# Tile 0's keys from x by columns, centred by the mean's row, with 1/std applied behind the products

## The chip, the cores and the metric

The kernel runs on one core of one Trainium2 chip. The metric is the time of one launch on the device in microseconds (us), as the median of several runs. The engines of the core are TensorE (PE in the profile; PEld is its weight load), VectorE (DVE), ScalarE (ACT), GpSimd (POOL) and SyncE (SP), whose queue issues the DMAs of this kernel's early part. All times below that are not medians are on the clock of one profiled execution, counted from its first instruction.

## The reference, cut to what matters

The kernel computes x + A(layernorm(x)) + B(layernorm(x)) for 2048 tokens of width 512, where A is a linear attention block and B a mixture of experts with two experts of eight for each token. Only the keys and the gate's logits of A and B are touched here:

```python
def _layernorm(x, axis=-1, eps=1e-5):
    m = jnp.mean(x, axis=axis, keepdims=True)
    v = jnp.var(x, axis=axis, keepdims=True)
    return (x - m) / jnp.sqrt(v + eps)
...
xn = _layernorm(x, axis=-1)
...
phi = lambda t: jnp.where(t > 0, t + 1, jnp.exp(t)) + 1e-6
pq, pk = phi(q), phi(k)                       # k = xn @ wqkv[:, 512:1024]
kv = jnp.einsum("bhsd,bhse->bhde", pk, v)
z = jnp.einsum("bhsd->bhd", pk)
...
logits = xf @ w_gate                          # xf = xn
```

Since (x - m) / std times a weight is ((x - m) times the weight) / std for each token, the division by std may stand behind the product.

## The kernel before

The 2048 tokens are 16 tiles of 128 (`t` = 0 to 15). The first stage runs over the tiles on all engines at once. For a tile, DVE takes mean and variance (`ln_stat`: `bn_stats` into `bs`, then `bn_aggr` into `mv`); POOL adds epsilon and raises to the power -1/2 (`ln_pow`) and refines that to 1/std with the bias -mean/std (`ln_fin_g`: six small operations on `sm`, ending in `rs` and `nb`); ACT writes the normalized tokens `xn` (`ln_out`); PE transposes them to columns (`transp_pe`, tile `xtp`), and ACT and DVE split the columns into a rounded high part and a low rest (`transp_split`, tile `xnT`: `split_hi` on ACT, line 150, `split_lo` on DVE, line 153). PE then takes keys and logits from them in 24 products, three for each quarter of the width and each half of the weights (`k_proj`), the features `pk` of the keys are formed, split in two (`pkhl`, beside `xnhl` for the tokens), and PE adds their outer product to four accumulators (`g_acc`, `gacc`, 12 products of 512 columns).

Tiles 4 to 15 already go another way: their columns come ready from a transposed copy of x in memory (`xcols`, tile `xraw`), PE turns the means into a row (`means_pe`, tile `mrow`), DVE subtracts that row (`centre`), and ACT multiplies the products by `rs` as it forms the features. `TS` = 4 is the first such tile; for the tiles below it the constants `rneg`, `std` and `estd` are set by memsets (lines 270 to 272), and `scales` works them out for the others.

Tile 0 is the head of the kernel and is written out by hand (lines 780 to 820). Until its columns are there PE runs small products on ones (`keep_warm`, line 231). Its statistics, `va` and 1/std come on DVE (`ln_stat(0)`, `ln_pow` line 301, `ln_fin(0)`), DVE makes its `xn` in two halves (line 336), PE transposes these (`first_pe`), ACT and DVE split them (`first_hi`, `first_lo`; the latter reads PSUM). The weights of the keys come in four quarters (`wkst`, four DMAs on SP behind those of x tiles 0 and 1) and are split as they land (`wk_hi` on ACT, `wk_lo` on DVE, both reading SBUF). The products for tile 0 are issued in an order written out in `k_part` ((quarter, pass) pairs; pass 0 is high by high, 1 takes the low weights, 2 the low columns): `k1` for the first half of the key columns, `k2` for the second half and the gate. `transp_pe(1)` and `transp_split(1)` are issued within `k2`, `transp_pe(2)` within `g_acc(0)` behind its first four products.

The order on each engine is the order of the calls: the schedule is manual, and an engine does not pass an instruction that waits. So on DVE the statistics of tile 2 (`ln_stat(2)`) stand between the low parts of the third and fourth weight quarter, and on POOL the operations of `ln_pow` and `ln_fin_g` for tiles 1, 2, 3 follow one another. SP's queue is in order too: the writes of `xn` to `xn_d` (line 338) stand in it as issued, and the loads of x tiles 4 and 5 behind those of tiles 0 and 1.

## Time and profile before

| | us |
|---|---|
| median of 3 runs | 824.85 (824.60 to 825.12) |
| the profiled execution, as timed | 825.74 |
| its span, first to last instruction | 824.0 |
| PE busy in the span | 816.3 (99%) |
| DVE, ACT, POOL busy | 679.1, 554.0, 265.3 |

How to read the profile: a row of a timeline gives the start and the duration of one instruction or of several merged ones (x4: four), its engine, line, operation, the tile it writes and those it reads, and in brackets how long its engine sat idle before it and what released it. Successive instructions of one engine can overlap by about 0.1 us, since the next one starts before the last has drained. A line such as 153 belongs to a helper, so the tiles tell which use it is. Ends of matmuls are modelled.

### The profile page before, as it was taken

What the parts mean: (1) busy time and instruction counts of PE and PEld (TensorE: products, weight loads), DVE (VectorE), ACT (ScalarE), POOL (GpSimd) and SP (SyncE); (2) the same over time, 40 slices, a digit from 0 to 9 for tenths busy, and PEclk for the clock granted to TensorE, in tenths of its full rate; (3) what the DMA queues carried; (4) which work ended last, traced back from release to release, by engine and by line L of the source; (5) the groups of instructions that cost most, each with busy time, mean ns of one, the idle gap of its engine ahead of it and who ended that gap; (6) DMA issues with size and microseconds to landing.
All of it is one profiled execution on the core that took longest, in us unless ns stands there. A gap on an engine that the chain in (4) does not pass through costs nothing. (4 is left out here: it accounts for less than half of the span.)

```text
span 824.0 us, 15861 instructions
## 1 busy us (share of the span) xinstructions
PE 816.3 (99%) x5359; PEld 744.6 (90%) x5359; DVE 679.1 (82%) x1415; ACT 554.0 (67%) x1167; POOL 265.3 (32%) x380
## 2 busy tenths in 40 slices
PE   8999999999999999999999999999999999999997
PEld 8899888888999999999999999999999998888886
DVE  7898889989989777877887888788888888987851
ACT  5687574458777566667776777677767777776750
POOL 5675243465310600042505340451217023411011
PEclk9999999999999999999999999999999999999999
DMA  4861044465855843474648455745656464549507
GB/s 168 282 228 67 30 163 170 128 202 184 260 178 147 209 137 103 144 196 126 144 133 235 116 126 159 207 110 151 167 172 153 146 170 113 121 131 235 134 4 176
DMA packets 105498, 128.22 MB, mean 156 GB/s; under 512 B 14590, under 2 KB 68606, under 8 KB 105382
## 3 DMA queue, kind: packets, MB, share of 16 engines
q1 hardware_dynamic: 91526, 106.95, 42.7%
q0 software_dynamic: 12880, 18.66, 12.0%
q10 hardware_dynamic: 1008, 1.57, 0.6%
q8 instruction: 43, 0.70, 0.4%
q14 instruction: 41, 0.34, 0.1%
HBM read 97.23 MB, written 31.22 MB: 156 GB/s over the span
## 5 line engine op out<-in xcount | busy, mean ns | idle before, releaser
L1261 POOL DMA_INDIRECT out_dram<-yo,sidx x22 | 35.2, 1601 | 276.8 <-DVE yo L1256 272.5
L1261 POOL DMA_INDIRECT out_dram<-yu,L x47 | 77.9, 1657 | 92.4 <-ACT yu L1354 60.8
L153 DVE TENSOR_TENSOR h<-hs,h 128x512 fp32r<-128x512 f32 (+7 forms) x112 | 78.5, 701 | 5.5 <-ACT h L150 5.1
L150 ACT ACTIVATE h<-hs 128x512 fp32r<-128x512 f32 (+7 forms) x112 | 72.3, 646 | 3.2
L1412 ACT ACTIVATE hs<-px 128x288 f32<-128x288 f32 (+7 forms) x54 | 21.1, 390 | 55.1 <-PE px L1404 53.3
L1427 ACT ACTIVATE hs<-hs 128x288 f32<-128x288 f32 (+7 forms) x54 | 23.0, 427 | 45.9 <-DVE hs L1426 44.1
L1431 DVE TENSOR_TENSOR hs<-px,hs 128x288 f32<-128x288 f32 (+7 forms) x54 | 23.4, 434 | 34.0 <-PE px L1404 33.0
L1426 DVE TENSOR_TENSOR hs<-pz,hs 128x288 f32<-128x288 f32 (+7 forms) x54 | 23.3, 431 | 32.7 <-PE pz L1404 30.4
L500 PE MATMUL gacc<-pkhl,xnhl 128*128 128x512 f32 x192 | 48.0, 396 | 0.1
L1128 POOL DMA_INDIRECT xg<-xn_d,gidx x37 | 41.7, 1126 | 19.8 <-issue 7.6
L500 PEld LDWEIGHTS gacc<-pkhl,xnhl 128*128 128x128 f32 x192 | 34.8, 188 | 7.6 <-DVE pkhl L480 0.9
L1260 POOL MEMSET spacer<- 1x1 f32 x69 | 37.9, 550 | 7.3 <-issue 7.3
L1432 ACT ACTIVATE hs<-hs 128x288 f32<-128x288 f32 (+7 forms) x54 | 22.8, 422 | 18.0 <-DVE hs L1431 16.2
L1504 POOL TENSOR_TENSOR pz<-pq,den 128x512 f32<-128x512 f32 x16 | 17.3, 1084 | 53.5 <-DVE den L1503 52.3
L1437 DVE TENSOR_TENSOR hs<-py,hs 128x288 f32<-128x288 f32 (+7 forms) x54 | 23.0, 425 | 13.5 <-PE py L1404 12.7
L1473 ACT ACTIVATE e_q<-qp,rneg 128x512 f32<-128x512 f32 x16 | 11.0, 688 | 32.6 <-PE qp L1464 29.1
L1422 ACT ACTIVATE hs<-px 128x288 f32<-128x288 f32 (+7 forms) x54 | 21.2, 392 | 16.4 <-PE px L1404 13.8
L1285 PE MATMUL y<-w_5h,h 128*128 128x512 f32 (+2 forms) x88 | 32.0, 394 | 0.0
L1285 PE MATMUL y<-w_1h,h 128*128 128x512 f32 (+2 forms) x88 | 32.0, 393 | 0.0
L1285 PE MATMUL y<-w_2h,h 128*128 128x512 f32 (+2 forms) x88 | 32.0, 393 | 0.0
L1285 PE MATMUL y<-w_3h,h 128*128 128x512 f32 (+2 forms) x88 | 32.0, 393 | 0.0
L1285 PE MATMUL y<-w_4h,h 128*128 128x512 f32 (+2 forms) x88 | 31.7, 393 | 0.0
(699 smaller groups left out, 3177.5 us busy)
## 6 DMA issues: line engine op xcount, KB each, us to landing
wst<-in_B_w_dram SPq DMA_DIRECT2D x196, 128.0 KB
wst<-in_B_w_dram SPq DMA_DIRECT2D x36, 512.0 KB
zz<-in_B_w_dram SPq DMA_DIRECT2D x27, 512.0 KB
xs_d<-xg SPq DMA_DIRECT2D x119, 64.0 KB
xq<-xs_d SPq DMA_DIRECT2D x28, 256.0 KB
x<-in_A_x_dram SPq DMA_DIRECT2D x21, 256.0 KB
xn_d<-xn SPq DMA_DIRECT2D x16, 256.0 KB
xraw<-in_xcols_dram SPq DMA_DIRECT2D x6, 512.0 KB
```

Source lines behind the costliest of these rows:

```text
L150: A.activation(hi, src, AF.Copy)
L153: V.tensor_tensor(lo, src, raw(hi), op=ALU.subtract)
L500: T.matmul(gacc[d], xnhl[:, a, d * P:(d + 1) * P], pkhl[:, b, :], start=(t == 0 and i == 0), stop=(t == NT - 1 and i == 2))
L1128: G.indirect_dma_start(out=raw(t), out_offset=None, in_=xn_d, in_offset=IOA(ap=gidx[:, b:b + 1], axis=0))
L1260: G.memset(spacer, 0.0)
L1261: st = G.indirect_dma_start(out=rows, out_offset=IOA(ap=idx, axis=0), in_=src, in_offset=None, compute_op=ALU.add).ins
L1285: T.matmul(ya[r, d][:m], h[a][:, d * P:d * P + m], w[b][:, n % 2, :], start=(first and i == 0), stop=(last and i == 2))
L1426: V.tensor_tensor(c12, pz_, c12, op=ALU.add)
L1427: A.activation(c12, c12, AF.Silu)
L1431: V.tensor_tensor(c22, px, c22, op=ALU.add)
L1432: A.activation(c22, c22, AF.Silu)
L1437: V.tensor_tensor(c11, pz_, c11, op=ALU.add)
```

## The change

The load of tile 0's columns (`xraw0`, half of the first entry of `xcols`) is put behind that of x tile 0, and the load of x tile 1 behind the first weight quarter. In the head, PE turns the mean of tile 0 into a row and DVE subtracts it from `xraw0` in place; `cols_hi(0)` and `cols_lo(0)` split the result. DVE's `va` and `ln_fin` for tile 0 go to POOL (`ln_fin_g(0, 1)`, between the statistics of tile 1 and the POOL work of tile 1). `xn` of tile 0 is made by ACT (`ln_out(0, 0, 0, A)`), behind the split of tile 1's columns, and with it the statistics and POOL work of tile 2 move behind that split. Keys and logits of tile 0 are multiplied by `rs` as ACT reads them (`k_act0`, `k_feat0`: Exp, Relu and Identity with a scale, in place of two Exp and a chain on DVE). The fourth weight quarter is split ahead of `ln_out(1)`, `transp_pe(1)` moves back by four products, the first run of small products is shortened from 136 to 112 and the second changed from 3 of 128 columns to 31 of 40. `rneg`, `std`, `estd` of tile 0 are worked out like those of the tiles from 4 on.

```diff
--- before.py
+++ after.py
@@ -174,13 +174,16 @@
     wk2 = [um(f"wk2_{i}")[:, :KC * 264].rearrange("p (k f) -> p k f", k=KC) for i in range(2)]
     wk_st = []
     load_x(0)
-    load_x(1)
+    xraw0 = wp.tile([P, SW], F32, tag="s", name="xraw0", bufs=18)
+    Q.dma_start(xraw0[:, :D], xcols[0, :, :D])
     for c in range(2):
         w = (512, 528)[c]
         for i in range(2):
             st = raw(um(f"wkst{c}{i}"))[:, :w]
             Q.dma_start(st, wkg[:, 1024 * c + w * i:1024 * c + w * i + w])
             wk_st.append(((wk1_v, wk2)[c], i, st.rearrange("p (k f) -> p k f", k=2)))
+            if c == i == 0:
+                load_x(1)
     load_x(2)
     load_x(3)
 
@@ -237,7 +240,7 @@
         idt = raw(um("idt"))[:, :P]
         make_identity(nc, idt)
         V.tensor_copy(ident_r, idt)
-        keep_warm("warm", 136, 40)
+        keep_warm("warm", 112, 40)
 
     def constants_b():
         def iota(t, pattern, base=0, cm=0):
@@ -267,9 +270,9 @@
         for r in range(E):
             G.memset(i_cap[:, RANKS[r]:RANKS[r] + 1], float(CAP[r]))
         G.memset(gate, 0.0)
-        G.memset(rneg[:, :TS], -1.0)
-        G.memset(std[:, :TS], 1.0)
-        G.memset(estd[:, :TS], 1e-6)
+        G.memset(rneg[:, 1:TS], -1.0)
+        G.memset(std[:, 1:TS], 1.0)
+        G.memset(estd[:, 1:TS], 1e-6)
         for a in range(4):
             G.memset(part[a * BLK:(a + 1) * BLK], float(a))
         G.affine_select(out=lower, in_=ones[:, :E * E].rearrange("p (a b) -> p a b", a=E),
@@ -298,7 +301,7 @@
         sm = wp.tile([P, 4, 2], F32, tag="sm", name=f"sm{g}", bufs=4)
         va, r0, t0, nb = (sm[:, j, :n] for j in range(4))
         rf = rs[:, g:g + n]
-        (V if g == 0 else G).tensor_scalar(va, mv[:, :n, 1], EPS, None, op0=ALU.add)
+        G.tensor_scalar(va, mv[:, :n, 1], EPS, None, op0=ALU.add)
         G.tensor_tensor(r0, va, eps_t[:, :n], op=ALU.pow)
         lnst[g] = (mv, va, r0, t0, nb, rf)
 
@@ -320,9 +323,10 @@
         G.tensor_tensor(nb, nb, rf, op=ALU.mult)
 
     def scales():
-        V.reciprocal(std[:, TS:], rs[:, TS:])
-        G.tensor_scalar(rneg[:, TS:], rs[:, TS:], -1.0, None, op0=ALU.mult)
-        G.tensor_scalar(estd[:, TS:], std[:, TS:], 1e-6, None, op0=ALU.mult)
+        for c in (slice(0, 1), slice(TS, NT)):
+            V.reciprocal(std[:, c], rs[:, c])
+            G.tensor_scalar(rneg[:, c], rs[:, c], -1.0, None, op0=ALU.mult)
+            G.tensor_scalar(estd[:, c], std[:, c], 1e-6, None, op0=ALU.mult)
 
     def ln_out(g, i, t, eng):
         mv, va, r0, t0, nb, rf = lnst[g]
@@ -436,14 +440,19 @@
 
     pks = {}
 
-    def k_feat0(k1, k2):
-        pk, e = ta("pk0"), ta("e_k0")
-        for o, src in ((0, k1), (256, k2[:, :256])):
-            A.activation(e[:, o:o + 256], src, AF.Exp)
-        V.tensor_scalar(e, e, 1.0, 1e-6, op0=ALU.min, op1=ALU.add)
-        for o, src in ((0, k1), (256, k2[:, :256])):
-            V.scalar_tensor_tensor(pk[:, o:o + 256], src, 0.0, e[:, o:o + 256], op0=ALU.max, op1=ALU.add)
-        V.tensor_copy(L[:, 0, :], k2[:, 256:264])
+    first = []
+
+    def k_act0(i, k):
+        if i == 0:
+            first.extend((ta("pk0"), ta("r0")))
+        for dst, fn in zip(first, (AF.Exp, AF.Relu)):
+            A.activation(dst[:, 256 * i:256 * i + 256], k[:, :256], fn, scale=rs[:, 0:1])
+
+    def k_feat0(k2):
+        pk, r = first
+        k_act0(1, k2)
+        A.activation(L[:, 0, :], k2[:, 256:264], AF.Identity, scale=rs[:, 0:1])
+        V.scalar_tensor_tensor(pk, r, 1.0, pk, op0=ALU.add, op1=ALU.min)
         pks[0] = pk
         return pk
 
@@ -465,7 +474,7 @@
     def z_add(t):
         G.tensor_tensor(zacc, zacc if t > 1 else pks.pop(0), pks.pop(t), op=ALU.add)
         if t == 6:
-            G.tensor_scalar(zacc, zacc, (NT - 1) * 1e-6, None, op0=ALU.add)
+            G.tensor_scalar(zacc, zacc, NT * 1e-6, None, op0=ALU.add)
 
     def two_hi(name, src, eps=False):
         hl = tb(name).rearrange("p (h c) -> p h c", h=2)
@@ -779,44 +788,50 @@
 
     constants_a()
     ln_stat(0, 0, 0)
+    m0 = psk("mrow0")[:, 0, :P]
+    T.transpose(m0, lnst_mv[0][:, 0, 0:1].broadcast_to([P, P]), ident)
+    keep_warm("warm_b", 31, 40)
+    xc[0] = xraw0[:, :D]
+    x3 = xc[0].rearrange("p (k c) -> p k c", k=KC)
+    V.tensor_tensor(x3, x3, m0.unsqueeze(1).broadcast_to([P, KC, P]), op=ALU.subtract)
     ln_pow(0, 1)
-    wk_hi(0)
     ln_stat(1, 0, 1)
+    ln_fin_g(0, 1)
     ln_pow(1, 1)
     ln_fin_g(1, 1)
-    ln_fin(0, 1)
-    ln_out(0, 0, 0, V)
-    first_pe()
-    keep_warm("warm_b", 3)
-    first_hi()
+    cols_hi(0)
+    wk_hi(0)
+    cols_lo(0)
     wk_lo(0)
-    first_lo()
     wk_hi(1)
     wk_lo(1)
     wk_hi(2)
     wk_lo(2)
     k1 = psm("acc", "k1_0", 256)
-    k_part(k1, wk1_v, (0, 0), (1, 0), (0, 1), (1, 1), (0, 2), (1, 2),
+    k_part(k1, wk1_v, (0, 0), (1, 0), (0, 2), (1, 2), (0, 1), (1, 1),
            (2, 0), (3, 0), (2, 2), (3, 2), (2, 1), (3, 1))
+    wk_hi(3)
+    wk_lo(3)
     ln_out(1, 0, 1, A)
+    k_act0(0, k1)
+    k2 = psm("acc", "k2_0", 264)
+    k_part(k2, wk2, (0, 0), (1, 0), (0, 2), (1, 2), (0, 1), (1, 1))
+    k_part(k2, wk2, (2, 0), (3, 0), (2, 2), (3, 2))
+    transp_pe(1)
+    transp_split(1)
+    k_part(k2, wk2, (2, 1), (3, 1))
+    ln_out(0, 0, 0, A)
     ln_stat(2, 0, 2)
     ln_pow(2, 1)
     ln_fin_g(2, 1)
-    wk_hi(3)
-    wk_lo(3)
-    k2 = psm("acc", "k2_0", 264)
-    k_part(k2, wk2, (0, 0), (1, 0), (0, 2), (1, 2), (0, 1), (1, 1))
-    transp_pe(1)
-    transp_split(1)
-    k_part(k2, wk2, (2, 0), (3, 0), (2, 2), (3, 2), (2, 1), (3, 1))
     load_x(4)
     load_x(5)
 
-    pk = k_feat0(k1, k2)
-    xnhl = (two_hi("xnhl0", xn[0]), two_hi("pkhl0", pk))
+    pk = k_feat0(k2)
+    xnhl = (two_hi("xnhl0", xn[0]), two_hi("pkhl0", pk, True))
     ln_out(2, 0, 2, A)
     two_lo(xnhl[0], xn[0])
-    two_lo(xnhl[1], pk)
+    two_lo(xnhl[1], pk, True)
     pend[0] = xnhl
     ln_stat(3, 0, 3)
     ln_pow(3, 1)
```

## Rows read from the trace of the kernel before

**Rows 1.** The page's first part, busy us of the engine, its share of the span and its instructions; then the granted TensorE clock in 40 slices of the span; then busy time by stretch (start:end, length, busy time and instructions of each engine, granted clock, share of DMA, GB/s).

```profile
PE 816.3 (99%) x5359; PEld 744.6 (90%) x5359; DVE 679.1 (82%) x1415; ACT 554.0 (67%) x1167; POOL 265.3 (32%) x380
...
PEclk9999999999999999999999999999999999999999
...
0.00:50.00 50.00, 47.37 (x422) 43.09 (x423) 40.51 (x79) 32.99 (x57) 31.32 (x92) 1.00 0.66 226
50.00:824.00 774.00, 768.89 (x4940) 701.48 (x4938) 638.64 (x1337) 521.01 (x1111) 233.97 (x289) 1.00 0.55 151
```

**Rows 2.** The waits of PE after 46 us: who waited for whom, us in total, times, longest.

```profile
PE pz L1404 <- ACT hs L1418: 0.4, 1, 0.4
PE kvp L940 <- DVE GT L153: 0.3, 1, 0.3
```

**Rows 3.** The timeline of the first 12 us: the statistics, the first weight quarter, and the chain to PE's first key products and to those of tile 1.

```profile
3.72 0.69 DVE L293 BATCH_NORM_STATS2 bs<-x 128x6 f32<-128x512 f32 x1 [1.99 <-DMA x<-in_A_x_dram]
4.45 0.18 DVE L294 BATCH_NORM_AGGREGATE mv<-bs 128x2 f32<-128x6 f32 x1
...
4.73 0.68 DVE L293 BATCH_NORM_STATS2 bs<-x 128x6 f32<-128x512 f32 x1
...
5.41 0.63 ACT L150 ACTIVATE wk1h<-wkst 128x512 fp32r<-128x512 f32 x1 [3.30 <-DMA wkst<-in_wkg_dram]
...
6.58 0.76 PE L412 MATMUL xtp<-ident_r,xn 128*128 128x128 f32 x4 [1.14 <-DVE xn L336]
...
7.81 0.52 PE L428 MATMUL k<-wk1h,xnT 128*128 128x256 f32 x2 [0.31 <-ACT xnT L150]
...
8.74 0.68 DVE L153 TENSOR_TENSOR wk1l<-wkst,wk1h 128x512 fp32r<-128x512 f32 x1
...
9.01 0.80 ACT L331 ACTIVATE xn<-x,sm,rs 128x512 f32<-128x512 f32 x1
9.34 0.70 DVE L153 TENSOR_TENSOR wk<-wkst,wk 128x528 fp32r<-128x528 f32 x1
...
11.18 0.60 ACT L150 ACTIVATE xnT<-xtp 128x512 fp32r<-128x512 f32 x1 [0.84 <-PE xtp L349]
...
11.87 0.70 PE L423 MATMUL k<-wk1h,xnT 128*128 128x256 f32 x4
```

**Rows 4.** The same timeline where the change's new operations have their like: PE's transposes of two rows of means, the subtraction of such a row on two tiles at once, the high part of columns that lie in SBUF, and ACT's reads of the products with a scale.

```profile
24.09 0.38 PE L368 MATMUL mrow<-ident_r,mv 128*128 128x128 f32 x2
...
27.28 1.20 DVE L376 TENSOR_TENSOR xraw<-xraw,mrow 128x1024 f32<-128x1024 f32 x1
...
28.52 0.63 ACT L150 ACTIVATE xnT<-xraw 128x512 fp32r<-128x512 f32 x1 [1.72 <-DVE xraw L376]
...
33.20 0.67 ACT L454 ACTIVATE pk<-k,rs 128x512 f32<-128x512 f32 x1
```

**Rows 5.** POOL's timeline between 5.7 and 8.8 us (the chain for tile 1), and the row of DVE that runs beside its later part.

```profile
5.73 0.26 POOL L301 TENSOR_SCALAR sm<-mv 128x1 f32<-128x1 f32 x1 [0.24 <-DVE sm L307]
6.07 0.57 POOL L302 TENSOR_TENSOR sm<-sm,eps_t 128x1 f32<-128x1 f32 x1
...
8.07 0.19 POOL L318 TENSOR_SCALAR sm<-sm 128x1 f32<-128x1 f32 x1
8.34 0.19 POOL L319 TENSOR_TENSOR rs<-sm 128x1 f32<-128x1 f32 x1
...
8.06 0.75 DVE L153 TENSOR_TENSOR xnT<-xtp,xnT 128x256 fp32r<-128x256 f32 x2 [0.62 <-ACT xnT L150]
```

**Rows 6.** DVE's timeline, and then POOL's, between 55 and 59 us, where both have work without a gap.

```profile
56.38 0.69 DVE L153 TENSOR_TENSOR xnT<-xraw,xnT 128x512 fp32r<-128x512 f32 x1
56.99 0.69 DVE L153 TENSOR_TENSOR xnhl<-xn,xnhl 128x512 fp32r<-128x512 f32 x1
57.59 0.69 DVE L459 SCALAR_TENSOR_TENSOR pk<-r,pk 128x512 f32<-128x512 f32 x1
...
56.60 0.55 POOL L316 TENSOR_SCALAR sm<-mv 128x2 f32<-128x2 f32 x1
57.12 0.60 POOL L317 TENSOR_TENSOR sm<-sm 128x2 f32<-128x2 f32 x1
57.81 0.52 POOL L318 TENSOR_SCALAR sm<-sm 128x2 f32<-128x2 f32 x1
58.41 0.20 POOL L319 TENSOR_TENSOR rs<-sm 128x2 f32<-128x2 f32 x1
```

**Rows 7.** The timeline of the way of tile 2 in the kernel before, from its statistics to its transposes within `g_acc(0)` and to its own key products.

```profile
9.95 0.69 DVE L293 BATCH_NORM_STATS2 bs<-x 128x6 f32<-128x512 f32 x1
...
10.95 0.60 POOL L301 TENSOR_SCALAR sm<-mv 128x1 f32<-128x1 f32 x1 [2.14 <-DVE mv L294]
...
13.79 0.64 POOL L320 TENSOR_TENSOR sm<-sm,rs 128x1 f32<-128x1 f32 x1
...
14.46 0.82 ACT L331 ACTIVATE xn<-x,sm,rs 128x512 f32<-128x512 f32 x1
...
14.81 1.07 PE L500 MATMUL gacc<-pkhl,xnhl 128*128 128x512 f32 x4
...
15.72 0.60 PE L349 MATMUL xtp<-ident_r,xn 128*128 128x128 f32 x4
...
18.01 0.28 PE L423 MATMUL k<-wk1h,xnT 128*128 128x256 f32 x1
```

## The prediction

> **What bounds the kernel now.** I read the page's first part and the busy time by stretch first, to see which engine sets the end: PE is busy 816.3 us of 824.0, and from 50 us on 768.89 of 774.00 [rows 1]. The waits of PE then say whether anything behind the head gives slack: after 46 us there are two, 0.4 and 0.3 us [rows 2]. So from the first key products to the end PE is the bound, and a shift of its work in the head is carried to the last instruction nearly whole. The head is where PE still idles (47.37 busy of the first 50 us, 2.6 us lost [rows 1]), so the timeline of the first 18 us is the view that decides, engine by engine, in the order of the calls. The reader should follow three moments there: the first key product at 7.81, the first product of tile 1 at 11.87 [rows 3], and tile 2's transposes at 15.72 with its first product at 18.01 [rows 7].
>
> **The first key product comes earlier.** Mean and variance of tile 0 are there at 4.45 + 0.18 = 4.63 [rows 3]. PE turns one row of means: two take 0.38 us [rows 4], and I take 0.3 for one. `xraw0` is the second load, in the place of x tile 1, whose statistics began at 4.73 without a wait [rows 3], so it is there. DVE's subtraction takes half of 1.20 us [rows 4] and some start, 0.66: from 5.0 to 5.7. ACT's `cols_hi(0)` takes 0.63 [rows 4], `wk_hi(0)` as much, started 0.5 behind it: 6.87. The first product starts at 6.9 in place of 7.81, a gain of 0.9 us. The run of 112 small products and the 31 behind cost nothing: PE waits there in either kernel.
>
> **x of tile 1 is later.** It is the fourth load now. The first landed at 3.72, the third at 5.41 [rows 3] (each released a waiting engine), 0.85 us a load; the fourth is worked out as 6.25. DVE, idle from 5.7, takes the statistics then: 6.3 to 7.2 with the aggregation (0.69 and 0.18). That holds `cols_lo(0)` behind it to 7.15. DVE then has five low parts in a row (tile 0's columns and four weight quarters), started 0.60 apart (8.74 to 9.34 [rows 3]), ending at 7.83, 8.43, 9.03, 9.64 and 10.25. By these PE takes its third product at 7.9, its fifth at 8.45, ends `k1` near 9.6 and the tenth product of `k2` near 10.75 (0.12 each). Up to here PE is not behind the kernel before, which began tile 1's transposes in the middle of `k2` near 10.5.
>
> **POOL's chain for tile 1 goes through that row of low parts.** This is the term that turns the sign. Eight POOL operations lie between the variance of tile 1 and its bias `nb`, without which ACT cannot write `xn` of tile 1. Alone they take about 2.5 us: 0.26 and 0.57 for the first two, steps of 0.27 for the six [rows 5]. In the kernel before they ran at 5.73 to 8.80, for the most part beside DVE work that reads one operand from PSUM (`first_lo` at 8.06, POOL's rows beside it still 0.19 us [rows 5]). Beside DVE operations with both operands in SBUF it is otherwise: between 56.6 and 58.4 each POOL operation takes 0.52 to 0.60 us and ends 0.04 to 0.08 behind the DVE instruction that was running, one for one; the next, beside no such work, takes 0.20 [rows 6]. The change puts tile 0's columns into SBUF, so all five low parts are of that kind. Beginning at 7.25: first operation to 7.87, the power to 8.43 + 0.57 = 9.0, the third to 9.68, the fourth to 10.29, the other four at 0.27 to 11.37. Without any such wait it would be 7.25 + 2.5 = 9.75. I take the waits, since the rows show them one for one. The work moved to POOL for tile 0 (eight operations, 4.7 to 7.2) is done just before, in time for `k_act0`, and costs nothing; were x of tile 1 earlier, it would stand in front of the chain all the same.
>
> **Tile 1's products come later.** `ln_out(1)` takes 0.80 [rows 3]: 11.41 to 12.21. `k_act0(0)`, `ln_out(0)`, the fourth quarter's work being done, are queued behind it on ACT, and nothing else in the queue would have helped. PE has stood since about 10.75. Transposes 0.60 [rows 7]: to 12.85. ACT's high part 0.60 [rows 3], behind the two reads of `k1`: 12.9 to 13.5. First product of tile 1 at 13.55, against 11.87: 1.7 us late. `k2`'s last two products fit into the wait.
>
> **Tile 2's tokens come later still.** Its statistics, before at 9.95 on DVE [rows 7], now follow the low part of tile 1's columns: 13.55 to 14.23, then 14.15 to 15.06 for the statistics. From statistics' end to `nb` the chain took from 10.95 to 13.79 + 0.64 = 14.43 in the kernel before, its first and last operation held up to 0.60 and 0.64 [rows 7]: 3.5 us. Now DVE has the feature of tile 0 and two low parts in that time, all three with both operands in SBUF, so 15.1 + 3.45 = 18.54 (alone 2.5: 17.6). `ln_out(2)`, 0.82 [rows 7], to 19.38. PE meanwhile does tile 1's 24 products in 14.81 - 11.87 = 2.94 us and the first four of `g_acc(0)` in 0.91 to the transposes' start [rows 3, 7]: 13.55 + 3.85 = 17.4. It then waits 2.0 us for `xn` of tile 2, which the kernel before had ready; the eight other products of `g_acc(0)` and all of tile 2 are queued behind that wait. `pkhl0`, worked through in the same way (ACT's second pair of reads to 14.87, DVE to 15.68, ACT to 16.45), is there at the end of tile 1's products and adds nothing. Transposes of tile 2 at 19.42 against 15.72: 3.7 us late. Behind them the order is as before, and tile 2's products follow at about 19.42 + 2.29 = 21.7 (18.01 before); its columns' low part is worked out as 21.8, in time for the third product.
>
> **What costs nothing.** ACT's four scaled reads in halves, the logits' read and `ln_out(0)` (0.67 for a whole read with a scale [rows 4], 0.80 for `ln_out` [rows 3]) are about 1.5 us more on ACT than before, all inside ACT's waits of the two paragraphs above; if the chains were quick, ACT would hold tile 1's columns to about 11.9, no gain on 11.87. DVE is relieved by 1.4 us there. The stores of `xn` move on SP's queue to 12.3 and 14.3, and the loads of x tiles 4 and 5 behind them to about 14.6; their statistics come near 24, over 9 us later, and the kernel's first load is in use 3.72 us after the span's start [rows 3], so nobody waits. Three more tiny operations in `scales` and a slot more of the `s` tiles for `xraw0`, which may tie later tiles to other slots, I put at 0, between -0.4 and +0.4, the longest wait of PE that the later kernel shows [rows 2].
>
> **The sum.** +3.7 us. The profiled execution was timed at 825.74, its span 824.0; it would read 829.4. Against the median of 824.85 I forecast 828.6.
>
> **The clock.** In every row of before the granted clock is 1.00, the 2.4 GHz level, though PE idled 1.14 us before 6.58 [rows 1, 3]. After the change PE has more of such waits: up to 6.9, at 10.75 to 12.25 and at 17.4. If the clock fell to 1.2 GHz for tile 1's products and the first four of `g_acc(0)`, these 3.85 us would take 7.7, of which 2.0 lie in the wait for tile 2: +1.9 us more. The Trainium skill (TensorE: Matmul & The Clock Gate, Part 4) says that transposes do not count as busy for the gate in the way products do, which speaks for that rival, since transposes are what PE does between its waits here; no row of before shows a fall. By that rule the time is 830.5, by the rows 828.6.
>
> **The rivals.** First, POOL is not held up: if both chains took 2.5 us alone, tile 1 would start at 11.95 (ACT's queue), tile 2's statistics end at 13.5, `nb` at 16.0, the transposes at 16.87: +1.15, so 826.0. Rows 6 speak against it. Second, the end on the other side: the earlier start arrives. If tile 1 followed PE's 0.9 us gain and tile 2's tokens were ready behind the fourth product of `g_acc(0)`, the time were 824.85 - 0.9 = 823.95. That is decided at tile 2: from the first product of tile 1 to the place of its transposes PE has 3.85 us, in which DVE's low part and statistics (1.5), the chain and `ln_out` (0.8) must fit, so the chain would have to take 1.5 us; its shortest in the rows is 2.5. All the idle time in PE's head after the small products is about 1.6 us, so even a perfect head hardly reaches a gain of 0.2%. Third, the clock falls: 830.5. Fourth, the change does not do what it says: the first product isn't earlier since `xraw0` or the first weight quarter lands late; that moves the start but not the two chains, and gives the forecast's time.
>
> **How the numbers follow.** The forecast (with the fourth) 0.73, the clock's fall 0.12, POOL free 0.10, the early start that arrives 0.05. The range takes POOL's low bound and the clock's price: 826.0 to 830.8. A change under 0.2% (1.65 us, about what a measurement can tell from no change; 823.2 to 826.5) is what the second and first rivals give: 0.13. Slower by more 0.85, faster by more 0.02.
>
> **What would show it.** After the change: the first product of `k1` near 6.9; POOL rows of tile 1's chain at 0.5 to 1.0 us beside DVE's low parts, ending near 11.4; PE idle before tile 1's transposes, released by ACT's `xn`, about 1.5 us; PE idle within `g_acc(0)` before tile 2's transposes, about 2 us, released by `xn` again; the products of tile 2 near 21.7; from there on the same distances as before. Wrong I am if POOL's rows are 0.2 us beside the low parts, if DVE or ACT take another order than that of the calls, or if a stretch of the head shows a granted clock under 1.00.

## The result and the profile after

| | kernel before | changed kernel |
|---|---|---|
| median, us (4 executions each) | 824.99 (824.60 to 825.15) | 829.46 (829.13 to 830.77) |
| ratio, 95% interval (from the single executions) | | 1.0058 [1.0041, 1.0075] |
| the profiled execution, as timed | 825.74 | 829.65 |
| its span | 824.0 | 827.9 |
| PE busy in the first 50 us | 47.37 | 44.45 |

The change costs 4.5 us in the median, 4.8 by the ratio; 828.6 was forecast, in a range from 826.0 to 830.8. Busy time by stretch, with its columns as in [rows 1], shows first where that lies:

```profile
0.00:50.00 50.00, 44.45 (x392) 40.11 (x393) 35.65 (x63) 30.65 (x53) 28.92 (x93) 0.97 0.59 201
50.00:828.00 778.00, 773.49 (x4970) 705.87 (x4968) 643.73 (x1345) 524.97 (x1118) 237.48 (x297) 1.00 0.56 152
9.00:10.00 1.00, 0.90 (x8) 0.72 (x7) 1.00 (x3) 0.21 (x1) 0.92 (x2) 1.00 0.34 119
10.00:11.00 1.00, 1.00 (x7) 1.00 (x6) 0.44 (x1) 0.35 (x1) 0.88 (x3) 0.50 0.07 27
12.00:13.00 1.00, 0.98 (x5) 0.67 (x4) 0.03 (x1) 0.62 (x1) 0.27 (x2) 0.50 0.00 0
```

The head has lost 2.9 us of PE's work; behind 50 us PE is as full as before (99.4% of the stretch, 99.3 in [rows 1]). The third number from the end is the granted clock: 0.97 over the head, and 0.50, the 1.2 GHz level, from 10.0 to 13.4 us. The page's row of 40 slices shows only nines for it, since a slice there is 20.7 us long.

The timeline of the changed kernel's head answers to [rows 3, 5, 7]:

```profile
4.17 0.18 DVE L297 BATCH_NORM_AGGREGATE mv<-bs 128x2 f32<-128x6 f32 x1
...
4.89 0.46 PE L792 MATMUL mrow<-ident_r,mv 128*128 128x128 f32 x1
...
5.39 0.69 DVE L796 TENSOR_TENSOR xraw<-xraw,mrow 128x512 f32<-128x512 f32 x1 [1.03 <-PE mrow L792]
...
7.13 0.69 DVE L296 BATCH_NORM_STATS2 bs<-x 128x6 f32<-128x512 f32 x1 [1.06 <-DMA x<-in_A_x_dram]
7.31 0.50 PE L432 MATMUL k<-wk1h,xnT 128*128 128x256 f32 x2 [0.93 <-ACT wk1h L150]
...
8.13 0.57 POOL L304 TENSOR_SCALAR sm<-mv 128x1 f32<-128x1 f32 x1 [1.18 <-DVE mv L297]
8.54 1.29 DVE L153 TENSOR_TENSOR wk1l<-wkst,wk1h 128x512 fp32r<-128x512 f32 x2
...
8.78 0.87 POOL L305 TENSOR_TENSOR sm<-sm,eps_t 128x1 f32<-128x1 f32 x1
...
9.73 0.76 POOL L318 TENSOR_TENSOR sm<-sm 128x1 f32<-128x1 f32 x1
9.74 0.70 DVE L153 TENSOR_TENSOR wk<-wkst,wk 128x528 fp32r<-128x528 f32 x1
...
10.58 2.40 PE L432 MATMUL k<-wk,xnT 128*128 128x264 f32 x10
10.65 0.64 ACT L150 ACTIVATE wk<-wkst 128x528 fp32r<-128x528 f32 x1 [1.44 <-DMA wkst<-in_wkg_dram]
...
11.32 0.76 POOL L322 TENSOR_TENSOR rs<-sm 128x1 f32<-128x1 f32 x1
11.32 0.71 DVE L153 TENSOR_TENSOR wk<-wkst,wk 128x528 fp32r<-128x528 f32 x1 [0.88 <-ACT wk L150]
12.16 0.19 POOL L323 TENSOR_TENSOR sm<-sm,rs 128x1 f32<-128x1 f32 x1
12.38 0.81 ACT L335 ACTIVATE xn<-x,sm,rs 128x512 f32<-128x512 f32 x1 [1.09 <-POOL sm L323]
...
13.25 0.71 PE L353 MATMUL xtp<-ident_r,xn 128*128 128x128 f32 x4 [0.27 <-ACT xn L335]
...
14.65 0.74 PE L427 MATMUL k<-wk1h,xnT 128*128 128x256 f32 x4 [0.44 <-ACT xnT L150]
...
15.24 0.68 DVE L296 BATCH_NORM_STATS2 bs<-x 128x6 f32<-128x512 f32 x1
...
19.39 0.19 POOL L323 TENSOR_TENSOR sm<-sm,rs 128x1 f32<-128x1 f32 x1
...
19.61 0.81 ACT L335 ACTIVATE xn<-x,sm,rs 128x512 f32<-128x512 f32 x1 [2.10 <-POOL sm L323]
...
20.48 0.66 PE L353 MATMUL xtp<-ident_r,xn 128*128 128x128 f32 x4 [1.72 <-ACT xn L335]
...
22.80 0.28 PE L427 MATMUL k<-wk1h,xnT 128*128 128x256 f32 x1
```

The three moments that the prediction follows: the first product starts at 7.31 (7.81 before [rows 3]), so the change does what it says and gains 0.5 us; the first product of tile 1 at 14.65 (11.87 [rows 3]), 2.8 late; tile 2's transposes at 20.48 and its first product at 22.80 (15.72 and 18.01 [rows 7]), 4.8 late. Read the brackets backwards from there: PE waited 1.72 us for `xn` of tile 2; ACT, which writes it, waited 2.10 for POOL's last operation of tile 2's chain; that chain began behind statistics at 15.24, which stood behind the low part of tile 1's columns; and those came from an `xn` for which ACT had waited 1.09 on POOL's chain for tile 1.

The waits of PE, up to 46 us and then behind it:

```profile
PE xtp L353 <- ACT xn L335: 2.0, 2, 1.7
...
PE gacc L509 <- DVE pkhl L489: 0.5, 1, 0.5
```

The second one is at 107 us and has no like in the kernel before [rows 2]; the 0.4 us `pz` wait of [rows 2] is absent here. That wait belongs to the execution and not to the change: 3 of the 14 profiles have it, this one of the kernel before and two of kernels with the change. It cost PE more than its 0.4: the products of `y` ahead of it start at 287.82 before and 293.06 after, 5.2 late, those behind it at 289.74 and 294.31, 4.6 late, so 0.7 us were lost there in the kernel before. DVE's last sum (`xo`) starts at 824.61 against 820.01 before, 4.6 late; behind it the span goes on for 3.3 us against 4.0 (3.3 to 4.3 among all profiles), which makes 3.9 between the two spans.

### The profile page after: what moved, and what is told of

Read it like the earlier page. It is cut to its first block, busy times and chain, and to the rows that moved or that the text cites. A ratio compares the mean times of both kernels' runs of the same rounds, so it can differ in the third digit from the quotient of the medians.

```text
span 827.9 us, 15865 instructions
## 1 busy us (share of the span) xinstructions
PE 817.9 (99%) x5360; PEld 746.0 (90%) x5360; DVE 679.4 (82%) x1407; ACT 555.6 (67%) x1170; POOL 266.4 (32%) x389
## 5 line engine op out<-in xcount | busy, mean ns | idle before, releaser
L1143 POOL DMA_INDIRECT xg<-xn_d,gidx x37 | 42.1, 1137 | 20.7 <-DMA wst<-in_B_w_dram 6.9
```

The source lines that it names most:

```text
L1143: G.indirect_dma_start(out=raw(t), out_offset=None, in_=xn_d, in_offset=IOA(ap=gidx[:, b:b + 1], axis=0))
```

## The experiments

My theory: the time goes to two chains that the change has put one behind the other, POOL's work for tile 1 (held up by DVE's low parts) and the statistics, POOL's work and tokens of tile 2, which now start behind tile 1's. Rivals: PE's clock; the loads, one more of which now stands ahead of x of tile 1; something behind the head. All runs are listed here, and then told one by one. "Tile 1" and "tile 2" are the starts of their first key products in the profiled execution. The ratios are taken from the single executions and are not the quotients of the two medians.

| kernel | median, us (lowest to highest) | median of before beside it | ratio to the kernel before | tile 1 | tile 2 |
|---|---|---|---|---|---|
| before (profile of [rows 1 to 7]) | 824.85 (824.60 to 825.12) | | | 11.87 | 18.01 |
| changed | 829.46 (829.13 to 830.77) | 824.99 | 1.0058 [1.0041, 1.0075] | 14.65 | 22.80 |
| changed, again | 829.59 (828.99 to 830.49) | 825.18 | 1.0060 [1.0046, 1.0074] | 13.98 | 22.13 |
| tile 2's statistics early | 827.67 (827.26 to 828.99) | 825.39 | 1.0028 [1.0018, 1.0039] | 14.57 | 20.81 |
| before, tile 2's statistics late | 827.13 (826.65 to 828.01) | 825.39 | 1.0024 [1.0015, 1.0033] | 11.77 | 20.03 |
| tile 1's refinement on DVE | 830.60 (829.91 to 831.28) | 825.39 | 1.0065 [1.0051, 1.0079] | 13.21 | 21.39 |
| the same, again | 829.21 (828.70 to 830.14) | 824.73 | 1.0052 [1.0038, 1.0066] | 13.09 | 21.25 |
| both repairs | 828.00 (827.32 to 829.14) | 825.55 | 1.0035 [1.0022, 1.0049] | 12.86 | 19.08 |
| both, more small products | 827.74 (827.06 to 828.72) | 825.18 | 1.0033 [1.0021, 1.0045] | 13.04 | 19.27 |
| both, tile 1 ahead of the last quarter | 828.69 (827.41 to 830.08) | 825.18 | 1.0043 [1.0029, 1.0057] | 13.91 | 20.88 |
| more small products alone | 830.80 (829.75 to 831.75) | 825.39 | 1.0062 [1.0048, 1.0076] | 15.84 | 23.99 |
| x of tile 1 third | 828.91 (828.41 to 829.98) | 825.55 | 1.0042 [1.0028, 1.0056] | 14.88 | 23.05 |
| both, more small products, no extra load | 826.46 (826.12 to 826.95) | 824.73 | 1.0016 [1.0007, 1.0025] | 12.68 | 18.92 |
| the same, `scales` of tile 0 apart | 826.21 (825.88 to 826.66) | 824.92 | 1.0014 [1.0005, 1.0023] | 12.69 | 18.93 |

**Tile 2's statistics early.** One part of the change undone: statistics and POOL work of tile 2 stand again behind the last low part of the weights.

```diff
     wk_hi(3)
     wk_lo(3)
+    ln_stat(2, 0, 2)
+    ln_pow(2, 1)
+    ln_fin_g(2, 1)
     ln_out(1, 0, 1, A)
...
     ln_out(0, 0, 0, A)
-    ln_stat(2, 0, 2)
-    ln_pow(2, 1)
-    ln_fin_g(2, 1)
```

> The changed kernel with tile 2's statistics and POOL work issued ahead of tile 1's ln_out, behind the fourth weight quarter's low part, where DVE stands idle. The chains (forecast): tile 2's transposes no longer wait 1.7 us for xn, PE runs through g_acc(0), tile 2's products start near 21.1 in place of 22.8; 827.7, against 829.5 for the changed kernel. The clock (rival): the loss is the stretch at half clock around 10 to 13 us and stays; 829.5.

Measured: 827.67. The timeline of this kernel, tokens and transposes of tile 1, then tokens, transposes and first product of tile 2:

```profile
11.71 0.81 ACT L335 ACTIVATE xn<-x,sm,rs 128x512 f32<-128x512 f32 x1 [0.82 <-POOL sm L323]
...
12.83 1.05 PE L353 MATMUL xtp<-ident_r,xn 128*128 128x128 f32 x4
...
17.34 0.80 ACT L335 ACTIVATE xn<-x,sm,rs 128x512 f32<-128x512 f32 x1
...
18.53 0.60 PE L353 MATMUL xtp<-ident_r,xn 128*128 128x128 f32 x4
...
20.81 0.28 PE L427 MATMUL k<-wk1h,xnT 128*128 128x256 f32 x1
```

No bracket stands behind tile 2's transposes: the wait for tile 2 is gone, and the kernel is 1.8 us faster than the changed one (2.2 with each set against the kernel before beside it). Here too the clock was 0.50, from 7.6 to 14.4 us, and the median came out as the chains give it. In the profiled execution the fall was not free, though: `xn` of tile 1 was written by 12.52, but PE, still in `k2` at half clock, began its transposes at 12.83 and took 1.05 us for them (0.71 in the changed kernel).

**The same part in the kernel before.** There, only the three calls for tile 2 are moved behind the split of tile 1's columns.

```diff
-    ln_stat(2, 0, 2)
-    ln_pow(2, 1)
-    ln_fin_g(2, 1)
     wk_hi(3)
     wk_lo(3)
...
     transp_pe(1)
     transp_split(1)
+    ln_stat(2, 0, 2)
+    ln_pow(2, 1)
+    ln_fin_g(2, 1)
```

> The kernel before with one part of the change alone: the statistics and POOL work of tile 2 moved behind the split of tile 1's columns. The chains: statistics end near 13.3 in place of 10.86, bias near 16.5, ln_out to 17.3, transposes of tile 2 at 17.4 in place of 15.72; 1.7 us more than before, 826.7. If PE's place in g_acc(0) had slack or DVE's relief paid for it: 825.0 to 825.4.

Measured: 827.13, and in its timeline:

```profile
17.71 0.66 PE L349 MATMUL xtp<-ident_r,xn 128*128 128x128 f32 x4 [1.46 <-ACT xn L331]
...
20.03 0.28 PE L423 MATMUL k<-wk1h,xnT 128*128 128x256 f32 x1
```

One moved group of three calls, with nothing else of the change, makes the kernel before 1.7 to 2.0 us slower (medians; ratio), by the same wait. The granted clock was 1.00 in this execution. So this chain is shown from both sides: 2.0 us at tile 2's first product in either, 1.7 to 2.2 in the medians.

**Tile 1's refinement on DVE.** The six operations that follow the power go from POOL to DVE (four there), behind the low part of the second quarter.

```diff
     ln_pow(1, 1)
-    ln_fin_g(1, 1)
...
     wk_hi(1)
     wk_lo(1)
+    ln_fin(1, 1)
```

> The changed kernel with the refinement of tile 1's 1/std on DVE (four small operations behind the low part of the second weight quarter) in place of six on POOL. The chains: POOL's work ends with the power near 9.7, the bias is there near 10.5, so ln_out(1) follows the fourth quarter's high part at 11.25 in place of 12.38; tile 1 and all behind it 1.1 us earlier, 828.4. If POOL's chain was not what tile 1 waited for: no change, 829.5, or 0.5 us more for the work put on DVE.

Measured: 830.60, a miss, although the head did as expected: tile 1's first product 1.4 us earlier than in the changed kernel, tile 2's as well. Part of that is x of tile 1, which landed earlier: counted from the start of tile 1's statistics, its first product comes after 6.3 us here and 6.5 in the second run, against 7.5 and 7.2 in the changed kernel's two profiles, so the edit is worth 0.7 to 1.2 us in the head. A second run of it asks whether something behind the head takes this back.

> Tile 1's refinement on DVE, once more, since its head was 1.4 us shorter in the profiled execution and its time was not (830.6). If the time of this kernel follows its head: 828.2 to 828.8. If something behind the head takes the 1.4 us back in each execution: 830 or more again, and the profile shows a wait of PE behind 30 us of about that size that the changed kernel hasn't.

Measured: 829.21, above what the head gives and below what a loss in each execution gives; 4.5 over the kernel before beside it, as the changed kernel is. The profiled execution had its head shifted by 3.2 us against [rows 7], its last sum by 3.1 (823.15), and took 828.70; PE's only waits of 0.3 us or more behind 46 us were the 0.5 at `pkhl`, which the changed kernel has too, and the 0.3 of [rows 2]. In the first run's profile there was one more, 0.4 us for a gather (`xg`) near 176 us. So the profiled execution follows its head, and the median does not. The executions sort by their mean granted clock: 828.70 and 828.75 at 1.000 and 0.999, 829.21 to 830.14 at 0.998. An explanation that fits, but that no trace of this kernel shows: PE's weight load now waits only 0.17 us for tile 1's tokens, so a fall of the clock ahead of them delays tile 1, as it did in the profile of "tile 2's statistics early", and tile 2's statistics stand behind it; in the changed kernel the longer wait took it up (below).

**Both repairs.** The two edits above together.

> The changed kernel with both repairs: tile 2's statistics ahead of ln_out(1), and tile 1's refinement on DVE. The chains: the two gains add, 1.1 and 1.7 us, 826.7, which leaves about 1.7 us over the kernel before, for the loads that land later (x of tile 1, the fourth weight quarter) and hold ACT and DVE.

Measured: 828.00, 1.3 more than expected. In the profile tile 2's first product is 3.7 us earlier than in the changed kernel, at 19.08; the profiled execution was the fastest one, with 827.32. The head still stands 1.1 us behind the kernel before. So the two chains are most of the head's loss, but less of the time's: 2.5 us remain over the kernel before beside it. Against "tile 2's statistics early" the second repair brings tile 2 forward by 1.7 us in the profile and nothing in time (2.5 and 2.3 us over the kernel before; ratios 1.0035 and 1.0028), as it brought nothing when alone. What the first chain costs is thus shown in the head, and not in the time. The next runs look for the rest.

**The clock.** More small products: in the changed kernel 24 more in `warm_b`, 20 behind the first two key products, 40 ahead of tile 1's transposes; and, in another run, only the first of these three with both repairs.

```diff
-    keep_warm("warm_b", 31, 40)
+    keep_warm("warm_b", 55, 40)
```

> The changed kernel with more small products on ones in PE's waits (24 more ahead of the first key product, 20 behind the first two, 40 ahead of tile 1's transposes). The chains: the granted clock stays at 1.00 through the head, k2's first ten products take 1.2 us in place of 2.4, but PE then waits longer for xn of tile 1 and the time is the same within 0.3 us, 829.5. The clock: the time falls by the 1.2 us, 828.3.

> Both repairs, and 24 more small products ahead of the first key product. The chains: tile 2's first product near 19.1, 1.1 us over the kernel before. If the granted clock, which fell in some executions with both repairs alone, made up the rest of the 2.5 us they were slower, it now stays near 1.000 in every execution and the time is 1.1 to 1.6 us over the kernel before; if the rest lies elsewhere (the end, DMA), still 2.5 us over it.

Measured: 830.80 and 827.74. Four of five executions of the first had a mean granted clock of 1.000 and still took 829.75 to 831.23, about 5 us more than the kernel before: a full clock does not bring the time back. What the clock costs the run doesn't tell, since the small products can stand in the way themselves. In the profiled execution, the fifth, the clock fell all the same (11.1 to 14.5 us), x of tile 1 came late (its statistics at 7.80), and its `xn` was written by 13.61, but PE, in the last of the 40, began the transposes at 14.52. The second is as far above the kernel before beside it as both repairs are (2.6 and 2.5), at mean clocks of 0.998 to 1.000 in place of 0.996 to 1.000: the clock isn't most of the rest either, though the slowest executions of both (829.14 and 828.72) are at the lowest clock of each.

**The changed kernel again.** To see the clock's fall in another place:

> The changed kernel itself, to be compared with the two beside it on the same chip. Tile 2's first product near 22.8 in the trace as before, and a time 4.5 us over the kernel before, 829.9. Its profile also shows whether the stretch at half clock (10 to 13.3 us the first time) lies at the same place.

Measured: 829.59. Windows of PE's clock in this second profile (columns as above), and under them its timeline:

```profile
14.00:15.00 1.00, 1.00 (x5) 1.00 (x6) 1.00 (x2) 1.00 (x3) 0.00 (x0) 0.59 0.12 43
15.00:16.00 1.00, 1.00 (x7) 1.00 (x6) 0.96 (x3) 1.00 (x3) 0.44 (x1) 0.50 0.52 199
```

```profile
13.98 1.08 PE L427 MATMUL k<-wk1h,xnT 128*128 128x256 f32 x4 [0.45 <-ACT xnT L150]
...
18.48 1.07 PE L509 MATMUL gacc<-pkhl,xnhl 128*128 128x512 f32 x4
...
19.81 0.66 PE L353 MATMUL xtp<-ident_r,xn 128*128 128x128 f32 x4 [0.26 <-ACT xn L335]
```

Now the clock falls in tile 1's 24 products (14.2 to 17.6 us): they take 18.48 - 13.98 = 4.5 us, where the first profile has 17.64 - 14.65 = 3.0. But the wait for tile 2 has shrunk from 1.72 to 0.26, by 1.5 as well. In the first profile the fall lay in `k2`'s ten products (2.40 us; 1.37 here), and PE waited 0.27 for tile 1 behind them all the same. Where PE's work is followed by a longer wait for another engine, the fall is taken up by it; where it is not, as in "tile 2's statistics early", it is paid.

**The loads.** First, x of tile 1 as the third load, ahead of the first weight quarter:

```diff
     Q.dma_start(xraw0[:, :D], xcols[0, :, :D])
+    load_x(1)
...
-            if c == i == 0:
-                load_x(1)
```

> The changed kernel with x of tile 1 loaded third, ahead of the first weight quarter. The chains: x of tile 1 lands about 0.9 us earlier (near 6.2), and with it the variance, POOL's chain and tile 1's products, 828.6, though the first key product starts later (near 7.8 in place of 7.31). If the late landing of the fourth weight quarter (10.65), which stands ahead of ln_out(1) on ACT, is what holds tile 1: no change, 829.5.

Measured: 828.91. Its profile shows what was won at one place and lost at another: tile 1's statistics at 6.82, but the first weight quarter is split at 7.52 only, so that PE starts its first product at 8.21. The clock was at 0.50 from 7.2 to 14.1 us and held tile 1 besides: its `xn` was written by 12.41, its transposes began at 13.13. The run decides little. Second, with both repairs, `ln_out(1)` ahead of the last quarter's split, and the transposes of tile 1 ahead of `k2`'s last six products, so that the last quarter holds nobody up:

```diff
+    ln_out(1, 0, 1, A)
     wk_hi(3)
     wk_lo(3)
...
-    ln_out(1, 0, 1, A)
-    k_act0(0, k1)
...
-    k_part(k2, wk2, (2, 0), (3, 0), (2, 2), (3, 2))
     transp_pe(1)
     transp_split(1)
-    k_part(k2, wk2, (2, 1), (3, 1))
+    k_part(k2, wk2, (2, 0), (3, 0), (2, 2), (3, 2), (2, 1), (3, 1))
+    k_act0(0, k1)
```

> Both repairs, and on ACT ln_out(1) ahead of the fourth weight quarter's high part, tile 1's transposes and split ahead of k2's last six products and of k_act0(0), as the kernel before had them. The chains and the loads: ln_out(1) starts at the bias, 9.9, in place of 10.66; tile 1's first product near 12.1 (12.86 with both repairs), tile 2's near 18.3; 0.3 us over the kernel before, which is within what can be told from no change. If the loads alone hold tile 1: no better than with both repairs.

Measured: 828.69, a miss; in the profiled execution x of tile 1 came at 7.33 and the clock was at 0.50 from 9.1 to 12.6 us; `xn` of tile 1 was written by 11.52, but PE began its transposes at 12.62 and tile 1's first product at 13.91. Last, both repairs and the 24 small products without the extra load, x of tile 1 second as in the kernel before:

```diff
-    Q.dma_start(xraw0[:, :D], xcols[0, :, :D])
+    load_x(1)
...
-            if c == i == 0:
-                load_x(1)
...
-    V.tensor_tensor(x3, x3, m0.unsqueeze(1).broadcast_to([P, KC, P]), op=ALU.subtract)
+    V.tensor_tensor(x3, xt[0].rearrange("p (k c) -> p k c", k=KC), m0.unsqueeze(1).broadcast_to([P, KC, P]), op=ALU.subtract)
```

> Both repairs (tile 2's statistics early, tile 1's refinement on DVE) and 24 more small products, without the load of tile 0's columns: x of tile 1 is the second load again, and DVE centres x of tile 0 as it lies by rows. Left out is thus the reading of tile 0 by columns, so keys and logits of tile 0 are other numbers (what is issued is the same). If the extra load is what still keeps the two repairs above the kernel before: statistics of tile 1 right behind the centring, near 6.1 (6.5 to 7.1 with the load), the fourth weight quarter split by 9.8 (10.1 to 10.7 with it), tile 1's first product near 11.7, tile 2's near 17.9, and the time 824.9 to 825.6, no slower than the kernel before. If the loads are not the cause: tile 2's first product stays at 19.1 to 19.3 and the time at 827.5 to 828.

Measured: 826.46, between the two expectations. The timeline of this kernel:

```profile
5.99 0.69 DVE L294 BATCH_NORM_STATS2 bs<-x 128x6 f32<-128x512 f32 x1
...
6.97 0.55 POOL L321 TENSOR_TENSOR sm<-sm,rs 128x1 f32<-128x1 f32 x1
...
7.60 0.55 POOL L302 TENSOR_SCALAR sm<-mv 128x1 f32<-128x1 f32 x1
...
8.23 0.87 POOL L303 TENSOR_TENSOR sm<-sm,eps_t 128x1 f32<-128x1 f32 x1
...
9.13 0.16 DVE L308 SCALAR_TENSOR_TENSOR sm<-sm 128x1 f32<-128x1 f32 x1 [0.46 <-POOL sm L303]
...
12.68 0.74 PE L425 MATMUL k<-wk1h,xnT 128*128 128x256 f32 x4 [0.44 <-ACT xnT L150]
```

Tile 1's statistics start at 5.99 without waiting, and ACT has written the high parts of all four weight quarters by 8.95. Yet tile 1's first product is only 0.2 to 0.4 us earlier than with the load, not 1.2: its variance is there at 6.89, but POOL is busy with tile 0's chain until 7.52, and the first two operations for tile 1 then run beside low parts, 0.55 and 0.87 us. Tile 0's chain on POOL has taken the place of the late x. The time stands 1.7 us over the kernel before beside it (1.3 by the ratio), 0.7 to 0.8 less than with the load (2.5 and 2.6; 1.4 to 1.6 less by the ratios), and tile 2's first product moved by 0.2 to 0.4. The executions lie within 0.8 us (11 of them), at mean clocks of 0.999 and 1.000, where those with the load spread over 1.7 to 1.8 us. So the load costs some 0.7 us in the medians and up to twice that by the ratios, whose intervals still touch; part of it lies in the other executions rather than in the profiled ones.

**Behind the head.** The wait at 107 us. Near 88 us DVE's `pkhl` takes 0.46 us longer than in the kernel before (1.27 and 0.81), and DVE is that much later from there on; its rows and POOL's there, in the changed kernel:

```profile
85.55 0.53 POOL L329 TENSOR_SCALAR estd<-std 128x1 f32<-128x1 f32 x1
...
87.15 1.30 POOL L475 TENSOR_TENSOR zz<-zz,pk 128x512 f32<-128x512 f32 x1
87.73 1.27 DVE L489 SCALAR_TENSOR_TENSOR pkhl<-pk,pkhl 128x512 fp32r<-128x512 f32 x1
```

POOL's sum of tile 11's features (`zz`) starts behind the four operations of `scales`, two of them new, and DVE's `pkhl`, which reads two operands from SBUF, ends 0.55 us behind POOL's end. The run: without the load as above, and `scales` for tile 0's column ahead of tile 8's products.

```diff
-    def scales():
-        for c in (slice(0, 1), slice(TS, NT)):
+    def scales(*cs):
+        for c in cs:
...
     for t in range(3, NT):
+        if t == 8:
+            scales(slice(0, 1))
...
-                scales()
+                scales(slice(TS, NT))
```

> The kernel without the extra load (tile 0's columns still not read, so its keys and logits are other numbers), and in it scales works out tile 0's column five tiles earlier, ahead of the products of tile 8, alone on POOL, instead of together with the columns of the tiles from 4 on. In the changed kernel's profile the two more POOL operations of scales beside DVE's work (0.66 and 0.53 us) push the sum of tile 11's features on POOL to 87.15, into DVE's pkhl, which takes 1.27 instead of 0.81; DVE is 0.44 later from there on, and PE waits 0.5 us for pkhl before the last outer product. If that is the cause of the 0.5 us: pkhl near 0.8 there, no wait of PE for pkhl behind 46 us, and the time 0.5 less than without this edit, 826.0, at 1.2 over the kernel before. If it is not: the wait of 0.5 us is there again and the time stays at 826.3 to 826.6, 1.7 over.

Measured: 826.21. Its timeline at the same place:

```profile
82.84 1.30 POOL L473 TENSOR_TENSOR zz<-zz,pk 128x512 f32<-128x512 f32 x1 [0.58 <-DVE pk L466]
...
83.87 0.82 DVE L487 SCALAR_TENSOR_TENSOR pkhl<-pk,pkhl 128x512 fp32r<-128x512 f32 x1
```

`pkhl` takes 0.82, the wait at 107 us is gone, and PE's products of the routing counts behind it (`pos_ps`) start at 108.39 where the run without this edit has 108.79; at the end 0.25 of these 0.4 us are left (last sum at 820.50 and 820.75). The medians differ by 0.25, by 0.4 over the kernel before beside each, by 0.2 by the ratios, whose intervals overlap. So the mechanism is shown in the trace, and its worth, between 0.2 and 0.45 us, is no larger than what the medians can tell.

## Why the prediction was right

**Where the time goes** was right: all is lost in the head, PE stays full behind it, and the shift of tile 2's first product arrives at the end. In the profiles with the change's order of `scales`, the last sum is late by 0.1 to 0.2 us less than tile 2's first product (4.60 and 4.79; again 3.92 and 4.12; refinement on DVE, again, 3.14 and 3.24; statistics early 2.59 and 2.80), for these lack the `pz` stall, 0.7 us in the profile of before, and lose the 0.5 at 107 us.

**The first product** came 0.5 us earlier, not 0.9. PE's transpose of the means' row began 0.54 us behind the variance and took 0.46, where 0.3 was taken. The small products were not free, as the forecast had them: PE ran them without a gap until 4.86, and the transpose, queued behind them, began at 4.89, though the variance was there at 4.35. In the second profile they came 0.025 us apart in place of 0.033, the transpose began at 4.65, and with 6.91 the forecast's 6.9 was met.

**x of tile 1** is the mis-sized term. Worked out from a landing every 0.85 us, it was to be there at 6.25; its statistics began at 7.13, in the second profile at 6.75, and from 6.54 to 7.80 in the other kernels with this order of loads. The rate taken from the first three loads didn't hold for the fourth. This 0.9 us is most of the 1.1 by which the head is later than worked out; in the second profile x was 0.5 later than worked out, and tile 1 and tile 2 0.4.

**POOL's chain for tile 1** was right, its sign and size: worked out as 7.25 to 11.37, 4.1 us, it ran from 8.13 to 12.35, 4.2, with rows of 0.57, 0.87 and twice 0.76 us beside DVE's low parts. In the four other profiles with this chain on POOL in the changed order it took 3.6 to 4.1; tile 0's eight operations, beside no low part, took 2.5 in the changed kernel (4.45 to 6.95). The rival by which POOL is not held up falls. The Trainium skill (SBUF — State Buffer, Who interferes with whom) says that a DVE instruction with two SBUF inputs contends with a GpSimd instruction that reads SBUF. These rows agree, against 0.19 to 0.26 us, and 0.57 for the power, beside nothing of the kind [rows 5]. That the size fits so closely is in part luck: the forecast has the fourth of the eight held up, and here it was the seventh, for the low part of the last weight quarter came at 11.32, its load being late, and not before 10.25. One reading was wrong without harm: the kernel before did not run this chain for the most part beside work that reads PSUM. Its longest row stands beside a low part of the weights, and shows the same effect:

```profile
6.72 0.78 POOL L315 TENSOR_TENSOR sm<-sm 128x1 f32<-128x1 f32 x1
6.76 0.68 DVE L153 TENSOR_TENSOR wk1l<-wkst,wk1h 128x512 fp32r<-128x512 f32 x1
```

The wait of 1.5 us that the forecast has before tile 1's transposes was 0.27 in this profile, where the slower products of `k2` filled it, and 1.31 in the second. As said above, no run shows the price of this chain in the time.

**Tile 2's way** was right, and shown from both sides: from the end of its statistics at 16.14 to `nb` at 19.58 it took 3.4 us (3.45 worked out), and PE waited 1.72 (2.0). Both experiments on it bear it out. What the prediction said of POOL's work for tile 0, that it would stand in front of tile 1's chain if x came earlier, is what the run without the load shows.

**The sum** of the head was 3.7; the profile has 4.8. That the spans differ by 3.9 is due to three smaller items: the `pz` stall absent (-0.7), the end behind the last sum (-0.7), and the wait at 107 us (+0.5). The first two are accidents of the executions, so it is luck that 3.9 lies so near to 3.7; the medians, 4.5 apart, are the better test, and they are not explained item by item. The last of the three is a step that failed: the more operations of `scales` were put at 0, between -0.4 and +0.4. They are small, but they delay a 1.30 us operation on POOL into DVE's way.

**The clock** fell, as the third rival has it, in both profiles, and one of the prediction's own signs of being wrong, a stretch of the head under 1.00, was thus there. Yet its time of 830.5 was not reached: the rival has 2.0 us of the slower products in the wait for tile 2, and all of what fell lay in such waits. On the rule about transposes these runs decide nothing: in the first profile the clock fell at 10 us with no transposes since 4.89, behind waits of 0.93 and 0.86 us; in the second one behind the transposes of tile 1.

**The start that arrives** (faster) was never near. Even with both repairs, no extra load and `scales` apart, 826.21 is above the kernel before. Of the 1.7 us by which the version with the stall at 107 us lies over it, the two profiled executions show 0.6 (826.31 and 825.74): 0.9 in the head, 0.5 at 107 us, and less by the `pz` stall (0.7) and the end (0.2). The rest is in the standard of comparison: the profiled execution of before took 0.9 us more than its median. The `pz` stall can be 0.7 of these; where the rest of them lies is open.

## What to carry to other kernels

A quicker start of a bound engine is worth only what the work queued behind it can follow: before moving a step, take the next tile, and the one after it, through every engine's queue, and count what their tokens now stand behind. A small operation on POOL is priced by what DVE does beside it, and a wait shows in the profile only where the order no longer hides it; moving three calls to another place in a hand-written order cost 1.7 to 2.0 us without one instruction more. A load's landing is read from a load in the same place in the queue; the gaps between the first ones do not carry over to the next.

## What was not expected of the hardware

- The clock of TensorE fell to 1.2 GHz at other places in two executions of one kernel: at 10.0 to 13.4 us in the one, 14.2 to 17.6 in the other, each time behind waits of PE of about 0.9 to 1.3 us. The kernel before, with a wait of 1.14 us [rows 3], kept 1.00, and so did the second run of tile 1's refinement on DVE, with waits of 1.12 and 0.75: these waits alone do not tell whether the clock falls.
- Where a load is added, the landing of the next one differs from execution to execution by over a microsecond (statistics of tile 1 at 6.54 to 7.80), and the last weight quarter comes 1.3 to 2.2 us later: ACT, waiting for it, split it at 9.76 to 10.65 in six profiles with the load, and at 8.50 in one without it.
- POOL holds DVE as DVE holds POOL: in three kernels `pkhl` ended 0.55 us behind the end of POOL's 1.30 us sum that had begun first (before, 83.76 and 83.21; changed, 89.00 and 88.45; `scales` apart, 84.69 and 84.14).
